# Stores ahead of casts on GpSimd, key casts later in one tile, and end stores on three queues, in a fused window-attention and MLP kernel

## The chip, the cores and the metric

The kernel runs on one core of one Trainium2 chip. The metric is device time in microseconds (us) of one execution; before the change it is 292.84, the median of three runs (292.73 to 294.62). A profiled execution of the same program took 293.94, of which the profile's span covers 292.2.

## The reference

What is computed is sliding-window attention over 8 batches of 8 heads (576 positions, 64 numbers per head, window of 32 to each side), followed by a two-layer network with a GELU on the 4608 tokens of 512 numbers that the attention gives. All inputs and the output are float32.

```python
scores = scale * np.matmul(q, k.transpose(0, 1, 3, 2))        # 8 x 8 x 576 x 576
mask = np.abs(pos[:, None] - pos[None, :]) <= 32
scores = np.where(mask, scores, -1000000000.0)
attn = softmax(scores)
x = np.matmul(attn, v).transpose(0, 2, 1, 3).reshape(4608, 512)
h = x @ w_in                                                  # 512 x 2048
g = 0.5 * h * (1.0 + np.tanh(c * (h + 0.044715 * h * h * h)))
return g @ w_out                                              # 2048 x 512
```

## The kernel before

The network's work is cut into nine tiles of 512 tokens, t = 0 to 8, and the attention into eight batches of 576 positions. They are interleaved by hand: while tile t's second product (`ffn_out`) runs on TensorE, the attention of batch b = t + 1 is placed between its matmuls, and the tile's first product with its GELUs (`ffn_in`, `in_mixed`) comes before it. Nothing is scheduled by a planner that weighs costs; each engine works off its instructions in the order in which the program records them, and a wait holds up everything behind it on that engine.

A tile's `ffn_out` is 112 matmuls, i = 0 to 111, in seven products n = 0 to 6 of 16 matmuls (a Strassen-Winograd scheme with seven products instead of eight). After the last matmul of a product VectorE (DVE) combines it into the output tile `yo`, at lines L804 (n = 0), L806 (n = 1), L808 (2), L816 (3), L819 or, in the last tile, L822 (4), L825 (5) and L834 (after n = 6). There is one `yo` for all tiles from 1 on, so a tile's L804 and L806 overwrite what the tile before has still to store. Rows 2 and 3 of `yo` are stored after L825, rows 0 and 1 after L834, by `store` (L755). A row is 128 tokens and is cut where its addresses in the output break, so one call gives two to five DMAs. All but the last tile's stores are issued by GpSimd (POOL); the last tile's go by SyncE (SP) and ScalarE (ACT), in turn within a call. In the built program SP's and ACT's DMAs use eight completion semaphores in turn, all POOL's another eight; a DMA waits until the one before it on its semaphore has landed. At its very end SP waits for the last use of each semaphore in a list.

The attention's steps are placed by tables, `PLAN` and its variants: each entry gives, for a matmul index i, the steps to record before it. `s0` to `s4` are scores of a head pair (4: the tails of all pairs, positions 480 to 575), `m` their masks (L511), `g`/`v` the sums and the products with the values, `x` the spread into `xT`, `a0` to `a3` the casts of the next batch's queries (L431) and `b0` to `b3` those of its keys (L441). After `b1` and `b3` SP issues a DMA transpose of two pairs of keys (L443). The mask of group 3, `m3`, stands at i = 70, that of the tails, `m4`, at 74, and the sums of groups 2 and 3, `g2`, at 88. Tile 0 has its own plan, tiles 1, 2 and 3 have `PLAN_1`, `PLAN_2` and `PLAN_L`, and tiles 4 to 6 have `PLAN`, in which `b0 b1` stand at i = 66 and `b2 b3` at i = 80. In `PLAN_L` they stand at 84 to 95.

Batch 3's values are loaded by SP into `vr` (L416) and cast by POOL into `V` in four casts (L1040), recorded in tile 1 before matmul 94; DVE pairs them (L236, L237) in tile 2 before they are used. The end of tile 1's product n = 5, and with it L825 and the stores of rows 2 and 3, comes at i = 95. At i = 98 batch 3's queries are cast (`open_and_turn`) and POOL casts its tail of queries and keys (L362, `cast_tails`). TensorE transposes that tail (L367, `trans_tails`) after column 12 of tile 2's first product, and ACT copies the result out (L369, L371). Columns 0 to 2 (`begun`) of a tile's first product are done at the end of the tile before.

Of the kernel before, what the change touches and what calls it, by code (L numbers as in the profile page):

```python
# [36 lines left out]
def cut(b):  # L37
# [8 lines left out]
PLAN = {7: "s0@0 s1@1 v-1", 16: "m0 m1 x-1", 35: "s2@0 g0@1", 38: "m2", 46: "x0 a0", 52: "x1 a1 a2 a3",  # L46
        63: "s3@0 s4@1", 66: "b0 b1", 70: "m3", 74: "m4", 80: "b2 b3", 88: "g2@1", 108: "x2", 112: "x3"}
# [5 lines left out]
PLAN_0 = {4: "s0@0", 9: "r1@1", 14: "s1@0", 15: "w1", 16: "m0", 19: "k2", 22: "r2@1", 23: "m1", 28: "s2@0 w2",  # L53
          29: "t-1@1", 34: "s-1@1 n0@0", 35: "e0", 36: "m2", 37: "k3", 38: "w5", 39: "m-1", 41: "w3 r3@1", 43: "e1 d0",
          47: "s3@0 v-1@1 d1 w4 e2 e3", 48: "d2 m3 d3", 50: "u3", 52: "x-1", 54: "n2@0",
          59: "p0@0 p2@1 x0 x1", 60: "e4 x2 x3", 61: "c1"}
# [12 lines left out]
PLAN_2 = {7: "s0@0 s1@1 v-1", 16: "m0 m1 x-1", 35: "s2@0 g0@1", 38: "m2", 46: "x0", 52: "x1",  # L69
          63: "s3@0 s4@1", 66: "a0 a1", 70: "m3", 74: "m4", 80: "a2 a3", 88: "g2@1", 108: "x2", 112: "x3"}  # L70

PLAN_L = {7: "s0@0 s1@1 v-1", 16: "m0 m1 x-1", 35: "s2@0 g0@1", 38: "m2", 46: "x0", 52: "x1",
          63: "s3@0 s4@1", 66: "a0 a1", 70: "m3", 74: "m4", 80: "a2 a3", 84: "b0", 88: "g2@1", 92: "b1", 95: "b2 b3", 108: "x2", 112: "x3"}

PLAN_1 = {12: "s0@0 s1@1 s2", 16: "m0 m1", 36: "m2", 56: "s-1@0 g0@1", 62: "m-1 x0", 64: "x1",
          80: "s3@0 g-1@1", 81: "m3", 90: "x2", 92: "x-1", 104: "v3 s4@1", 112: "x3 m4"}
# [6 lines left out]
LONE = 3  # L83
# [5 lines left out]
def kernel(  # L89
# [9 lines left out]
    nc = tc.nc  # L99
    B, H, S, D = q.shape  # L100
# [258 lines left out]
    def cast_tails(b, copy, half=slice(0, 128)):  # L359
        if len(halfs[b]) < 3:  # L360
            halfs[b].append(hp.tile([128, H, 64], FP16, name="t16", tag="t16"))
        copy(halfs[b][2][half, :, :], raws[b][2][half, :, :])  # L362
# [383 lines left out]
    def store(t, t4, yo, cols=slice(0, 512), *engs):  # L746

        m = i = 0
        while m < 128:
            b, c = divmod(t * 512 + t4 * 128 + m, S)  # L750
            q0, n = (0, cut(b)) if c < 4 * cut(b) else (cut(b), 144 - cut(b))
            j, p = divmod(c - 4 * q0, n)
            e = min(n - p, 128 - m)
            eng = engs[i % len(engs)] if engs else nc.gpsimd
            eng.dma_start(out_v[b, j, q0 + p:q0 + p + e, cols], yo[m:m + e, cols])  # L755
            m += e
            i += 1
# [16 lines left out]
    def ffn_out(t, i):  # L774

        n, blk, f = i // 16, i // 8 % 2, i % 8
        if n == 1 and t >= NT - 2:
            blk, f = divmod(i % 16, 4) if i % 16 < 8 else (i // 2 % 2, i // 4 % 4 * 2 + i % 2)
        a, w, new = WINO[n]
        end = t == NT - 1  # L780
        if i % 16 == 0 and new:
            pys[n % 2] = bank((1 + n) % 2)
            if end and n == 4:
                pys["apart"] = psO.tile([128, 512], FP32, name="py2", tag="O")
        py = pys[n % 2].rearrange("p (b c) -> p b c", b=2)
        apart = end and blk and n in (4, 6)
        if a[0] == "A":
            r0, c0 = 8 * (int(a[2]) - 1) + f, 256 * (int(a[1]) - 1) + 128 * blk
            lhsT = gTs[t][:, r0, c0:c0 + 128]
        else:  # L790
            lhsT = wino[a][:, f, 128 * blk:128 * blk + 128]
        one = end and n in (4, 6)
        nc.tensor.matmul(pys["apart"][:, 0:256] if apart else py[:, blk, :], lhsT,  # L793
                         wino[w][:, f, :], start=(new and i % (8 if one else 16) == 0),
                         stop=(i % (8 if one else 16) == (7 if one else 15)),
                         skip_group_check=True)
        if i % 16 < 15:
            return
        yo, left, right = wino["yo"], slice(0, 256), slice(256, 512)
        C11, C12, C21, C22 = (yo[:, r:r + 2, c] for r in (0, 2) for c in (left, right))  # L800

        M1, U2, U3 = C21, C12, C22
        if n == 0:
            (nc.scalar.copy if t >= NT - 2 else nc.vector.tensor_copy)(M1, py)  # L804
        elif n == 1:
            nc.vector.tensor_tensor(U2, py, M1, op=ALU.add)  # L806
        elif n == 2:
            nc.vector.tensor_copy(C11, py)  # L808
            if t >= NT - 2:
                for step in "z1 z2 z3".split():  # L810
                    sums(t, int(step[1]), PARTS[step[0]])
            if end:
                for x in range(2):
                    store(t, x, yo[:, x, :], left, nc.sync)
        elif n == 3:
            nc.vector.tensor_tensor(U3, py, M1, op=ALU.add)  # L816
        elif n == 4:
            if not end:
                nc.vector.tensor_tensor(C22, py, U3, op=ALU.add)  # L819
            else:  # L820
                for x, part in enumerate((py[:, 0, :], pys["apart"][:, 0:256])):
                    nc.vector.tensor_tensor(C22[:, x, :], part, U3[:, x, :], op=ALU.add)  # L822
                    store(t, 2 + x, yo[:, 2 + x, :], right, nc.sync, nc.scalar)
        elif n == 5:
            nc.vector.tensor_tensor(C21, py, M1, op=ALU.add)  # L825
            for x in range(2):
                store(t, 2 + x, yo[:, 2 + x, :], *((left, nc.sync, nc.scalar) if end else ()))

    def ffn_last(t):
        py = pys[0].rearrange("p (b c) -> p b c", b=2)  # L830
# [144 lines left out]
    for t in range(NT):  # L975
        b = t + 1
        att = b < B
        if t:
            for fc in range(begun):
                ffn_in(t, fc, 3, 4, then=False)  # L980
            for fc in range(begun):
                gelu(t, fc)
            if b == 2:
                open_and_turn(2)
                combine(2, nc.vector)
                combine(3, nc.vector)
            elif att:
                if t >= LONE:
                    in_x(t)
                if b == 3:  # L990
                    turn_keys(b)
            if t >= NT - 2:
                if t == NT - 2:
                    in_x(t)
                in_mixed(t)
            elif t >= LONE:
                in_mixed(t)
            for fc in range(begun, NF if t < LONE else 0):
                ffn_in(t, fc)
                if t == 1 and fc == 3:  # L1000
                    turn_keys(2)
                    load_vr(2)
                    raws[2] = [None, None, raws[2][2], vrs[2], tailp.tile([64, H, 64], FP32, name="vt", tag="vt")]
                    nc.sync.dma_start(raws[2][4], v[2, :, 512:S, :].rearrange("h p d -> p h d"))
                    raws[3] = rawp.tile([128, H, 256], FP32, name="qr", tag="q0")
                    load_q(3, raws[3])
                    combine(4, nc.vector)
                if t == 1 and 6 <= fc < 10:
                    cast_v(2, fc - 6)
                if t == 1 and fc == 6:  # L1010
                    trans_tails(1, psO.tile([128, 8, 128], FP16, name="pt", tag="O"))
                if t == 1 and fc == 8:
                    cast_tails(2, nc.scalar.copy)
                if t == 1 and fc == 13:
                    trans_tails(2, psO.tile([128, 8, 128], FP16, name="pt", tag="O"), copy=nc.scalar.copy,
                                copy_q=nc.scalar.copy)
                if t == 2 and fc == 12:
                    trans_tails(3, psO.tile([128, 8, 128], FP16, name="pt", tag="O"), copy=nc.scalar.copy,
                                copy_q=nc.scalar.copy)
                if t == 2 and fc == 8:  # L1020
                    pair_v(b, nc.vector.tensor_copy)
                if t == LONE - 1 and fc in (8, 9, 10, 11):
                    in_w(nc.vector, "B", (8, 9, 10, 11).index(fc) + 1)
        plan = PLAN_0 if not t else PLAN_1 if t == 1 else PLAN_2 if t == LONE - 1 else PLAN_L if t == LONE else PLAN if att else {16: "v-1", 40: "x-1"} if t == B - 1 else {}

        def group(g):
            return (b, g) if g >= 0 else (b - 1, 4)
# [6 lines left out]
        for i in range(113 if t else 65):  # L1034
            if t > 1 and i == {2: 40, 3: 56}.get(t, 4) and b + 1 < B:
                nc.gpsimd.tensor_copy(after, KLs[b % 2][:, 3, 0:1])
                load_v(b + 1)
            if t == 1 and i == 94:
                for c in range(4):
                    nc.gpsimd.tensor_copy(Vs[1][:, c, :, :], vrs[3][:, c, :, :])  # L1040
            if t == 1 and i == 98:
                open_and_turn(3)
                cast_tails(3, nc.gpsimd.tensor_copy)
            for act in plan.get(i, "").split():
                kind, at = act[0], int(act[act.index("@") + 1:]) if "@" in act else None
                g = int(act[1:].split("@")[0])
# [128 lines left out]
```

## Time and profile before

| | us |
|---|---|
| median of three runs | 292.84 (292.73 to 294.62) |
| profiled execution | 293.94 |
| its span | 292.2 |
| tile 1, L804 to L834 | 70.3 to 86.4 |
| tile 2, L804 to L834 | 101.5 to 116.2 |
| tile 4, L804 to L834 | 162.0 to 177.6 |
| last tile, DVE's last L834 | ends 288.33 |

The times of the tiles are where DVE's combining steps stand in the timeline. PE is TensorE's matmuls and PEld its weight loads, which overlap them; a small q behind an engine's name is its sequencer, which issues DMAs and waits for semaphores. In the timeline a line gives start and length in us, engine, line of the kernel, operation, what is written and read, how often, and in brackets the idle time of the engine before it and what ended that. In the chain of waits a line gives start, length and what was being done. In the rows by slices each digit is a fortieth of the span, 7.3 us.

The costliest groups of instructions are the matmuls of the first product (L600, 113.9 us in two groups), those of the second (L793), POOL's issues of stores (L755, 42.0 us in 77) and ACT's exponentials (L502, 29.5 us in 31). Of 36.70 MB read and 9.44 MB written, 97839 of 113792 packets are under 512 B.

### The profile page before, as it was taken

To read this page: it belongs to the slowest core of one execution; us is meant where nothing else is said; L and a number is where in the kernel's file an instruction comes from. 1 tells how busy PE (TensorE), PEld (TensorE's weight loads), DVE (VectorE), ACT (ScalarE), POOL (GpSimd) and SP (SyncE) were. 2 spreads that over 40 slices of the span, in tenths; PEclk is the share of its full clock that TensorE was granted. 3 is DMA by queue.
4 is the path that set the end of the run, shared out by engine and by line. 5 is a ranking of instruction groups with operands and counts; after the bars stand their busy time and mean duration, and the time that the engine had idled before them with its cause. 6 is when DMAs were issued, how large, how long until landed. Compare 5 with 4: busy or idle time off the path is not lost.

```text
span 292.2 us, 7443 instructions
## 1 busy us (share of the span) xinstructions
PE 283.3 (97%) x2993; PEld 197.0 (67%) x2993; DVE 225.5 (77%) x499; ACT 196.9 (67%) x323; POOL 92.7 (32%) x158
## 2 busy tenths in 40 slices
PE   8889999999999999999999989999999999999994
PEld 3535544557765677668866876688667877887783
DVE  4755377998897968798998778889888967875682
ACT  5875867878577865687658845895689577905800
POOL 3435324102318652505166108500800070016000
PEclk9999999999999999999999999999999999999999
DMA  7999998999999999869999998698820031005013
GB/s 219 276 372 399 358 311 201 246 195 187 272 222 195 261 217 192 220 156 217 134 185 248 179 162 185 193 180 126 186 45 2 2 87 61 0 3 144 0 43 103
DMA packets 113792, 51.01 MB, mean 175 GB/s; under 512 B 97839, under 2 KB 109615, under 8 KB 113502
## 3 DMA queue, kind: packets, MB, share of 16 engines
q1 hardware_dynamic: 89604, 38.77, 59.0%
q0 software_dynamic: 23088, 10.82, 23.1%
q10 hardware_dynamic: 1066, 0.96, 1.0%
q8 instruction: 23, 0.38, 0.6%
q14 instruction: 11, 0.09, 0.1%
HBM read 36.70 MB, written 9.44 MB: 158 GB/s over the span
## 4 chain that ended last, share of the span: by engine, by line
PE 82%; DMA 9%; SPq 5%; issue 1%; DVE 1%; POOL 0%; ACTq 0%; DVEq 0%
PE mm L793 29%; PE ph L600 17%; PE mm L600 14%; PE pu L656 7%; DMA kr<-in_k_dram 3%; PE ps_s L489 3%; PE py L765 3%; PE mm L765 2%; DMA wst<-in_moe_w_in_dram 2%; SPq L204 2%; DMA qr<-in_q_dram 2%; DMA V<-in_v_dram 1%; PE ps_od L516 1%; SPq L282 1%; PE ps_d L516 1%
## 5 line engine op out<-in xcount | busy, mean ns | idle before, releaser
L600 PEld LDWEIGHTS <-w_in 128*128 128x128 f16 x448 | 50.2, 113 | 39.6 <-POOL w_in L261 1.2
L755 POOL DMA_DIRECT2D out_dram<-y x77 | 42.0, 554 | 93.2 <-DVE y L825 75.3
L600 PE MATMUL ph<-xT,w_in 128*128 128x512 f16 x240 | 60.4, 379 | 0.6 <-POOL w_in L261 0.6
L793 PEld LDWEIGHTS <-s 128*128 128x128 f16 x512 | 49.4, 98 | 6.6 <-issue 0.4
L600 PE MATMUL mm<-xT,w_in 128*128 128x512 f16 x208 | 53.5, 379 | 0.0
L793 PE MATMUL mm<-t,s 128*128 128x256 f16 x376 | 44.9, 273 | 0.2 <-DVE y L806 0.2
L793 PEld LDWEIGHTS <-gT 128*128 128x128 f16 x384 | 36.2, 98 | 6.6 <-issue 0.3
L502 ACT ACTIVATE pe<-ps_s 128x960 f16<-128x960 f32 (+1 forms) x31 | 29.5, 974 | 14.2 <-PE ps_s L489 14.1
L793 PE MATMUL mm<-w_out,gT 128*128 128x256 f16 x256 | 32.6, 273 | 0.0
L741 DVE TENSOR_TENSOR s<-gT 128x512 f16<-128x512 f16 x64 | 26.9, 425 | 5.7 <-ACT gT L608 2.9
L608 ACT ACTIVATE gT<-mm 128x512 f16<-128x512 f32 x28 | 16.5, 599 | 21.6 <-PE mm L600 21.5
L608 ACT ACTIVATE gT<-ph 128x512 f16<-128x512 f32 x38 | 20.9, 606 | 6.6 <-PE ph L600 6.6
L114 ACT ACT_TABLE_LOAD x18 | 23.1, 1283 | 2.2 <-issue 1.9
L554 ACT ACTIVATE lt<-lt 128x480 f32<-128x480 f32 (+3 forms) x36 | 21.1, 585 | 1.1
L511 DVE TENSOR_TENSOR pe<-pe,band 128x960 f16<-128x960 f16 x28 | 18.1, 664 | 2.0 <-ACT pe L502 1.9
L704 ACT ACTIVATE gT<-ph 128x512 f16<-128x512 f32 x22 | 13.2, 600 | 4.8 <-PE ph L600 4.7
L793 PE MATMUL mm<-t,gT 128*128 128x256 f16 x128 | 16.2, 273 | 0.0
L526 PEld LDWEIGHTS <-V 128*64 128x64 f16 x520 | 12.6, 112 | 5.2 <-DVE V L237 1.3
L741 DVE TENSOR_TENSOR s<-s,gT 128x512 f16<-128x512 f16 x32 | 14.4, 450 | 1.1
L553 ACT ACTIVATE lt<-ps_od 128x480 f32<-128x480 f32 (+2 forms) x13 | 7.1, 546 | 11.6 <-PE ps_od L526 6.2
L793 PE MATMUL mm<-w_out,s 128*128 128x256 f16 x120 | 14.6, 273 | 0.0
L227 POOL DMA_DIRECT2D V<-in_v_dram x16 | 14.3, 912 | 0.5 <-PE mm L600 0.2
(153 smaller groups left out, 472.7 us busy)
## 6 DMA issues: line engine op xcount, KB each, us to landing
kr<-in_k_dram SPq DMA_DIRECT2D x31, 256.0 KB
qr<-in_q_dram SPq DMA_DIRECT2D x6, 1024.0 KB
wst<-in_moe_w_in_dram SPq DMA_DIRECT2D x8, 512.0 KB
vr<-in_v_dram SPq DMA_DIRECT2D x12, 256.0 KB
wst<-in_moe_w_out_dram SPq DMA_DIRECT2D x2, 1024.0 KB
wst<-in_moe_w_out_dram SPq DMA_DIRECT2D x4, 512.0 KB
V<-in_v_dram POOLq DMA_DIRECT2D x16, 128.0 KB, 8.2
qr<-in_q_dram SPq DMA_DIRECT2D x7, 256.0 KB
```

The costliest lines, as they stand in the source:

```text
L114: nc.scalar.add_instruction(mybir.InstLoadActFuncSet(name=nc.get_next_instruction_name(), act_func_set_id=which, ins=[], outs=[]))
L227: nc.gpsimd.dma_start(V[:, c, :, :], v[b, :, 128 * c:128 * c + 128, :].rearrange("h p d -> p h d"))
L502: nc.scalar.activation(pe, ps[:, :, 0:w], AF.Exp, scale=SCALE)
L511: nc.vector.tensor_tensor(pe, pe, m.rearrange("k (o j) p -> k o j p", o=1).broadcast_to(list(pe.shape)), op=ALU.mult)
L554: nc.scalar.activation(lt[:, 0:n], lt[:, 0:n], AF.Exp, scale=-1.0)
L600: nc.tensor.matmul(ph, w_cols[:, dc, fc // 4, fc % 4, :], xT[:, dc, t * 512 % RING:t * 512 % RING + 512], start=(dc == 0), stop=(dc == 3))
L608: nc.scalar.activation(gTs[t][:, fc, :], phs[fc], AF.Gelu_apprx_tanh)
L656: nc.tensor.matmul(ps[:, 256 * h:256 * h + 256], lhs[:, d, h, :], rhs[:, d, :], start=(n in (0, 2, 4) and h == d == 0), stop=(h == d == 1) ...
L741: nc.vector.tensor_tensor(dst, x, y, op=op)
L755: eng.dma_start(out_v[b, j, q0 + p:q0 + p + e, cols], yo[m:m + e, cols])
L765: nc.tensor.matmul(pys[t4], gTs[0][:, fc, t4 * 128:t4 * 128 + 128], w_out16[:, fc, :], start=new, stop=(fc == NF - 1))
L793: nc.tensor.matmul(pys["apart"][:, 0:256] if apart else py[:, blk, :], lhsT, wino[w][:, f, :], start=(new and i % (8 if one else 16) == 0) ...
```

## The change

It has three parts.

In tile 1 the four casts of batch 3's values move from i = 94 to i = 97, so that on POOL the four DMAs that store rows 2 and 3 of tile 1 (48, 80, 40 and 88 rows) come ahead of them. The cast of batch 3's tail moves from i = 98 of tile 1 into tile 2's first product, at column 3, so that on POOL it comes behind all stores of tile 1. The transposes of the tail move from after column 12 to after column 14.

Tile 4 gets a plan of its own, `PLAN_M`: `b0` moves from i = 66 to 84, `b1` to 92, `b2 b3` from 80 to 95. On DVE all four key casts then stand between L819 and L825; before, two stood ahead of the mask `m3` and two behind L819.

In the last tile the left halves of rows 2 and 3, after L825, go differently: row 2's two DMAs (40 and 88 rows) both by SP, row 3's five (32, 24, 24, 24, 24) by ACT and POOL in turn. Before, each row's were dealt to SP and ACT in turn.

Otherwise each engine's instructions and their order are the same; lines from L74 on move down by three, and later ones by up to six.

```diff
+PLAN_M = {7: "s0@0 s1@1 v-1", 16: "m0 m1 x-1", 35: "s2@0 g0@1", 38: "m2", 46: "x0 a0", 52: "x1 a1 a2 a3",
+          63: "s3@0 s4@1", 70: "m3", 74: "m4", 84: "b0", 88: "g2@1", 92: "b1", 95: "b2 b3", 108: "x2", 112: "x3"}
...
         elif n == 5:
             nc.vector.tensor_tensor(C21, py, M1, op=ALU.add)
             for x in range(2):
-                store(t, 2 + x, yo[:, 2 + x, :], *((left, nc.sync, nc.scalar) if end else ()))
+                store(t, 2 + x, yo[:, 2 + x, :],
+                      *((left, *((nc.scalar, nc.gpsimd) if x else (nc.sync,))) if end else ()))
...
-                if t == 2 and fc == 12:
+                if t == 2 and fc == begun:
+                    cast_tails(3, nc.gpsimd.tensor_copy)
+                if t == 2 and fc == 14:
                     trans_tails(3, psO.tile([128, 8, 128], FP16, name="pt", tag="O"), copy=nc.scalar.copy,
                                 copy_q=nc.scalar.copy)
...
-        plan = PLAN_0 if not t else PLAN_1 if t == 1 else PLAN_2 if t == LONE - 1 else PLAN_L if t == LONE else PLAN if att else {16: "v-1", 40: "x-1"} if t == B - 1 else {}
+        plan = PLAN_0 if not t else PLAN_1 if t == 1 else PLAN_2 if t == LONE - 1 else PLAN_L if t == LONE else PLAN_M if t == LONE + 1 else PLAN if att else {16: "v-1", 40: "x-1"} if t == B - 1 else {}
...
-            if t == 1 and i == 94:
+            if t == 1 and i == 97:
                 for c in range(4):
                     nc.gpsimd.tensor_copy(Vs[1][:, c, :, :], vrs[3][:, c, :, :])
             if t == 1 and i == 98:
                 open_and_turn(3)
-                cast_tails(3, nc.gpsimd.tensor_copy)
```

## The prediction, before the result was known

> **What bounds the kernel now.** First the page's busy times and slices:
>
> ```profile
> PE 283.3 (97%) x2993; PEld 197.0 (67%) x2993; DVE 225.5 (77%) x499; ACT 196.9 (67%) x323; POOL 92.7 (32%) x158
> ...
> PE   8889999999999999999999989999999999999994
> ...
> PEclk9999999999999999999999999999999999999999
> DMA  7999998999999999869999998698820031005013
> ```
>
> TensorE (PE) is busy 97% of 292.2 us at full clock and the chain of waits lies on it for 82%. An edit in the middle can gain only what PE loses to a wait; work shortened elsewhere is worth nothing. Listing PE's idle time from 60 us on leaves two gaps over 0.15 us, both DVE's doing, and then the end. The DMA row is full until 175 us, so a transfer put earlier pushes another.
>
> Gap one, the chain of waits at 153 to 177 us (start, length, what), tile 4:
>
> ```profile
> 157.83 3.96 SPq L204
> 161.79 0.04 issue
> 161.84 9.72 DMA kr<-in_k_dram
> ...
> 172.44 0.58 DVE pe L511
> 173.02 0.04 issue
> 173.06 0.39 PE ps_d L516 x2
> ```
>
> and DVE's timeline there:
>
> ```profile
> 169.70 0.69 DVE L816 TENSOR_TENSOR y<-mm,y 128x512 f32<-128x512 f32 x1
> 171.68 0.76 DVE L441 CAST k<-kr 128x512 f16<-128x512 f32 x2 [1.30 <-DMA kr<-in_k_dram]
> 172.36 0.65 DVE L511 TENSOR_TENSOR pe<-pe,band 128x960 f16<-128x960 f16 x1
> ```
>
> The key casts stand ahead of mask L511, so a mask whose scores ScalarE had exponentiated by 170.6 waits for keys that land at 171.56.
>
> Gap two, the timeline at 106 us (tile 2), POOL's at 87 to 99, and the DMA view's sizes with median us to landing:
>
> ```profile
> 105.84 0.69 DVE L806 TENSOR_TENSOR y<-mm,y 128x512 f32<-128x512 f32 x1 [1.95 <-DMA V<-in_v_dram]
> ...
> 106.59 0.38 PE L793 MATMUL mm<-t,s 128*128 128x256 f16 x2 [0.23 <-DVE y L806]
> ```
>
> ```profile
> 87.46 0.79 POOL L1040 CAST V<-vr 128x512 f16<-128x512 f32 x1 [5.85 <-DMA vr<-in_v_dram]
> ...
> 90.16 1.48 POOL L1040 CAST V<-vr 128x512 f16<-128x512 f32 x2 [0.36 <-DMA vr<-in_v_dram]
> 91.58 2.12 POOL L755 DMA_DIRECT2D out_dram<-y  x4
> ...
> 98.20 1.08 POOL L755 DMA_DIRECT2D out_dram<-y  x2 [0.90 <-DVE s L741]
> ```
>
> ```profile
> out_dram<-y POOLq DMA_DIRECT2D x1, 144.0 KB, 6.9
> ```
>
> L806 overwrites the output tile, so it waits for tile 1's stores, whatever load the profile names: the last one (72 rows, 144 KB) is issued at 98.75 and lands 6.9 us later, at 105.6.
>
> The end, SP's and ACT's last issues:
>
> ```profile
> 288.90 0.33 ACTq L755 DMA_DIRECT2D out_dram<-y  x1
> 289.26 0.32 SPq L755 DMA_DIRECT2D out_dram<-y  x1
> ```
>
> Their data are ready when DVE's last add ends, 288.33. SP waits 1.2 us more for the last landing (290.9), then works off its list of final waits; the span ends at 292.2.
>
> **Tile 4's keys late: -1.05 us.** Casts and their two transposes are kept; they move behind L819. Then: L816 ends 170.38, L511 and the tail's mask (0.65 and 0.55) end by 171.5, L819 (0.68; its matmuls end by 170.8) at 172.1, four casts at 0.34 us from one start to the next end at 173.5. The keys landed at 171.56, so they wait for nothing. PE's second sum, at 173.06, could start 0.22 us after the first (171.77, the spacing in tiles 3 and 5), at 171.99: 1.07 gained; I take 1.05. What is late next? L825, queued behind the casts: its matmuls would end at 174.94 - 1.07 = 173.87, the casts at 173.5, so 0.3 to 0.4 us of cover. The first key transpose on SP's queue follows the queries' one (ends 172.73) as now; the second goes at about 174.1 instead of 174.78. The next tile's scores come 17 us later. Bounds: 0, if the wait reappears at L825, to 1.19, the excess over the usual spacing of those starts.
>
> **Tile 2: -0.25 us net.** The four stores at L825 need only L825 (ends 83.34), so POOL, idle from 81.6 to 87.46, issues them at 83.6 and has 2.1 to 2.8 us of work (0.53 each here, 0.70 beside casts of DVE at 179 us): done by 86.4, before the first values land. Ahead of them in POOL's queue nothing waits; behind them are the casts. What it costs is DMA time: the queue is full, and 512 KB in the packets of these stores take 1.3 to 1.8 us of the 16 engines (the two 256 KB stores at 79.6 took 1.76). The four value loads, which landed at 87.4 to 90.8, thus come later by 0 to 1.8 us; I take d = 1.3, nearest the packets' undisturbed time. Casts end at 91.63 + d = 92.9. DVE's pairing copies of V, due at 94.12, still find them; SP's transposes behind the value loads slip by d too, and the first keys are needed only at 99.3 (landed 95.65), the second pair at 103 (98.82). Then seven stores (2.77 + 1.08 = 3.85) and only then the tail cast (0.61 to 0.88), which ends at 97.4 to 97.7. PE wants its four transposes after column 14, at 97.5 (97.72 less the 0.22 of transposes now at 95.77). Stall: 0 with d = 0, 0.7 with d = 1.8; I take 0.15. ScalarE's two copies out of them (0.37, 0.39) fit between its GELUs, idle 0.27 apart, and move the table load by at most 0.1.
>
> In return the 72-row store is issued at 95.0 + d and, even at 6.9 us, lands at 103.2, before L806 can start (103.89). PE's gap goes: 0.23 by the modelled ends, 0.40 by the weight load's idle time beside it; taken as 0.40. Net -0.25, from -0.4 to +0.5.
>
> **The end: -0.85 us.** Bytes and stores are the same, but the 11 DMAs after the last-but-one product (SP six, ACT five) become: SP 40, 88, 56, 48 rows; ACT 32, 24, 24, 72, 80; POOL 24, 24. In the built program the DMAs of SP and ACT share eight completion semaphores in turn, and each waits until the one eight before it has landed. Now the 48-row store goes at 289.26, held by a 24-row one issued at 287.23; the 80-row one goes at 288.90, held by the 88-row one issued at 286.88 (1.97 us before). With two DMAs gone to POOL's own semaphores the 48-row store depends on one issued at 285.67 and goes at 288.4 (data 288.33, SP has two issues fewer). The 80-row store depends on a 32-row one issued at 286.88; the 40-row one of that moment released its successor at 288.47, so 288.5 to 288.85. Last landing, 1.63 us after its issue as now (290.89 - 289.26): 290.2 to 290.5, or 290.85 with 1.97. Gain 0.45. Further, the last landing is now the first of SP's eight final waits, with seven behind it at 0.062 us; it becomes the eighth of nine, so 0.4 us less remains. Together 0.85, bounds 0.3 and 1.2. POOL's two stores are new here. DVE to POOL takes 0.3 us now (L825 ends 205.51, store 205.80): issues at 287.15 and 287.7; in the quiet stage at 262 us such stores land 1.9 to 2.7 us after issue, so by 290.4 at the latest, and SP waits for those first.
>
> The Trainium skill speaks against this part: "DMA: Bandwidth & Descriptors", Issuing engines are not separate DMA queues, says that DMAs from several engines run on the same 16 DMA engines and that this saves only the time to initiate them, usually small. By it the end would gain nearly nothing and the sum would be 1.3 (291.5); the trace disagrees so far, as waits for completions, and not only issuing, hold the last two.
>
> **Sum.** 1.05 + 0.25 + 0.85 = 2.15. The profiled execution took 293.94 (span 292.2 and 1.7 around it): 291.8 for it. It lies 1.10 above the median of 292.84, so 290.7 for the median. The shifts pass on: after both gaps the key loads start from casts that follow PE, and DMA has air at 120 to 127 and at 175 to 184 us, so nothing after them stays pinned to old times.
>
> **Rivals.** Tile 2 gives back more than it gets: d near 1.8, and PE stalls 0.7 at column 14. For it speaks the DMA share of 1.0 to 1.25 at 79 to 92 us; against it, POOL's stores share the engines and need not go first. That is +0.3 instead of -0.25: 291.3, chance 0.13.
>
> The transfers, not the issues, set the end: the 0.45 goes, and POOL's two stores take back part of the rest. Against it: the DMA share is 0.44 at 287 to 291 us. 291.2 to 291.6, chance 0.13.
>
> Tile 4's wait only moves: keys landing over 0.4 us later against PE make L825 late, and the adds behind it. Against it: tile 3 runs its casts in that place with no gap on PE. 291.4 to 291.8, chance 0.08.
>
> The two stalls are the profiled execution's own and hardly there in the median; then only the end remains: 292.0, chance 0.06.
>
> Slower than before: POOL's two stores land last. SP waits for them first, so with the 1.3 of the two tiles in hand a landing at 292.2 on the old clock (290.9 + 1.3; 4.5 us after the second issue) is where the change turns into a loss. At the full queue's 6.9 us it is 294.6, SP's end comes 3.7 later than now, and the time is 292.84 - 1.3 + 3.7 = 295.2. The quiet row (1.9 to 2.7) speaks against it. Chance 0.05.
>
> The forecast has 0.55, with 289.9 to 291.2 as its own range (all upper bounds together: 1.19 + 0.4 + 1.2 = 2.8). The range runs from 289.9 to 292.1 and leaves out the slower rival and mixtures. One per cent, what a measurement here can tell from no change, is 2.9 us: faster by more needs every part at its bound, 0.07; slower by more only the slow landing at its worst, 0.03; within, 0.90.
>
> **What would show it.** Right: in tile 4 DVE runs L511 directly after L816, L441 x4 after L819 without a wait, and the 0.90 gap before L516 is gone; L806 has no DMA wait; casts L1046 end at 92 to 93.5; the last SP issue lies at 288.3 to 288.5 on the old clock and POOL shows two issues after the last-but-one product. Wrong: a wait of L825 or of the transposes in column 14 over 0.5 us, or SP's final wait ending on POOL's stores.

## The result, and the profile after

The changed kernel takes 295.19 us (median of 22 runs, 293.96 to 297.10); the kernel before, in runs beside it, 293.96 (22 runs, 292.49 to 296.98). The ratio is 1.0042, 95% interval 1.0022 to 1.0061: about 1.2 us slower, where 2.15 faster was forecast. (The forecast's 290.7 was counted from a before of 292.84, so 1.1 of the 4.5 us from 290.7 to 295.19 is a difference between two medians of the kernel before.) The profiled execution took 294.83, of which the span is 293.1 (before 292.2). What follows goes through the same places as the prediction; lines from L74 on are 3 to 6 further down.

The page's busy times and slices. TensorE is as busy as before, so no work was added; two digits of its row differ from before: the 24th, at 168 to 175 us in tile 4, is 9 instead of 8, and the last is 1 instead of 4, which says that TensorE is done earlier relative to the span's end:

```profile
PE 283.1 (97%) x2993; PEld 196.8 (67%) x2993; DVE 225.6 (77%) x499; ACT 197.0 (67%) x323; POOL 94.4 (32%) x160
...
PE   8889999999999999999999999999999999999991
```

**Tile 4.** The chain of waits at 168 to 176 us (start, length, what), then VectorE's timeline:

```profile
169.31 2.84 PE mm L796 x25
172.14 0.32 PE ps_od L519 x2
172.46 0.20 PE ps_d L519 x2
...
173.13 2.73 PE mm L796 x24
```

```profile
170.00 0.69 DVE L819 TENSOR_TENSOR y<-mm,y 128x512 f32<-128x512 f32 x1
170.60 0.65 DVE L514 TENSOR_TENSOR pe<-pe,band 128x960 f16<-128x960 f16 x1
171.16 0.55 DVE L514 TENSOR_TENSOR pet<-pet,band 128x768 f16<-128x768 f16 x1
171.63 0.69 DVE L822 TENSOR_TENSOR y<-mm,y 128x512 f32<-128x512 f32 x1
172.23 1.43 DVE L444 CAST k<-kr 128x512 f16<-128x512 f32 x4
174.15 0.69 DVE L828 TENSOR_TENSOR y<-mm,y 128x512 f32<-128x512 f32 x1 [0.48 <-PE mm L796]
```

Before, the same last step stood at:

```profile
174.94 0.69 DVE L825 TENSOR_TENSOR y<-mm,y 128x512 f32<-128x512 f32 x1 [0.19 <-PE mm L793]
```

The chain no longer runs over the key loads, and the two sums (ps_od, ps_d) follow each other on TensorE without the gap. The mask runs directly after L819 and the four key casts wait for nothing; the step behind them, L828, waits for its matmuls only. From L819's start to L828's it is 4.15 us; before it was 5.24 (169.70 to 174.94): 1.09 gained.

**Tile 2.** GpSimd's timeline, then VectorE's at 104 us, then TensorE's at 98:

```profile
83.66 2.39 POOL L758 DMA_DIRECT2D out_dram<-y  x4 [1.35 <-DVE y L828]
...
92.16 0.88 POOL L1046 CAST V<-vr 128x512 f16<-128x512 f32 x1 [0.29 <-DMA vr<-in_v_dram]
92.99 3.98 POOL L758 DMA_DIRECT2D out_dram<-y  x7
96.97 0.98 POOL L365 CAST t<-tr 128x512 f16<-128x512 f32 x1
```

```profile
104.49 0.68 DVE L809 TENSOR_TENSOR y<-mm,y 128x512 f32<-128x512 f32 x1
```

```profile
98.00 0.40 PE L370 MATMUL pt<-idn,t 128*128 128x128 f16 x4 [0.48 <-POOL t L365]
```

The add that overwrites the output tile (L809, L806 before) waits for no store any more. But the casts of the values end at 93.04 instead of 91.64 and the tail cast at 97.95, so TensorE's transposes wait for it: 0.48 by the line's idle time, 0.65 by the distance of the starts over the usual one.

**The end.** The timeline from 285 us; SP's waits from 284 us on (waiting engine and line, released by: us in total, times, longest), after and then before; and the program's end on GpSimd by its source line (number of instructions: shortest, median and longest in ns, start of the first and of the last), after and then before:

```profile
286.35 1.00 POOL L758 DMA_DIRECT2D out_dram<-y  x2 [19.39 <-DVE y L828]
287.12 0.42 DVE L838 TENSOR_TENSOR y<-py,y 128x256 f32<-128x256 f32 x1 [0.45 <-PE py L796]
```

```profile
SPq L1175 <- PEq L1175: 2.9, 2, 2.4
SPq L1175 <- DMA out_dram<-y: 1.4, 1, 1.4
```

```profile
SPq L1170 <- DMA out_dram<-y: 1.2, 1, 1.2
...
SPq L1170 <- PEq L1170: 0.7, 2, 0.5
```

```profile
L1175 POOLq DRAIN  x3: 46/93/5564, 286.8 to 292.8; - x3
```

```profile
L1170 POOLq DRAIN  x3: 46/93/6027, 266.5 to 292.0; - x3
```

DVE's last add ends at 287.54 (before 288.33). SP's list of final waits is over at 290.02 (before 291.42), which is 2.48 after that add instead of 3.09. Then SP waits another 2.4 us, which the profile puts down to PE's sequencer, idle long before. The late one is GpSimd: at its own end stands a DRAIN, which begins at 286.8 and takes 5.56 us, to 292.33; the last barrier follows at 292.37. Before, the DRAIN began at 266.5, beside GpSimd's last stores, those of the tile before, and its 6.03 us were over at 272.56, under other work. So the span ends 5.56 after the last add, where it ended 3.91 after it before. GpSimd's two stores themselves landed at 288.46 and 289.25, ahead of the last landing of all, ScalarE's 80-row store at 289.86.

The three differences add up to the span's: +0.27 in tile 2, -1.09 in tile 4, +1.66 at the end, and with +0.03 ahead of them it is +0.87 in all (293.10 - 292.24, before rounding).

### The profile page after: what moved, and what is told of

Same layout as the page of the kernel before. It is cut to its first block, busy times and chain, and to the rows that moved or that the text cites. A ratio compares the mean times of both kernels' runs of the same rounds, so it can differ in the third digit from the quotient of the medians.

```text
span 293.1 us, 7444 instructions
## 1 busy us (share of the span) xinstructions
PE 283.1 (97%) x2993; PEld 196.8 (67%) x2993; DVE 225.6 (77%) x499; ACT 197.0 (67%) x323; POOL 94.4 (32%) x160
## 4 chain that ended last, share of the span: by engine, by line
PE 65%; POOL 1%; DVE 0%; issue 0%
PE mm L796 29%; PE ph L603 10%; PE mm L603 9%; PE pu L659 7%; PE ps_s L492 2%; PE ps_d L519 1%; PE mm L659 1%; PE ps_o L529 1%; PE ps_od L519 1%; PE ps_od L529 1%; PE py L796 1%; POOL out_dram L758 0%; POOL t L365 0%; DVE y L838 0%; PE pt L370 0%
## 5 line engine op out<-in xcount | busy, mean ns | idle before, releaser
L758 POOL DMA_DIRECT2D out_dram<-y x79 | 42.9, 551 | 111.4 <-DVE y L828 95.7
L492 PEld LDWEIGHTS <-KT 64*64 64x64 f16 x576 | 10.0, 106 | 6.1 <-issue 4.0
```

The costliest lines, as they stand in the source:

```text
L492: nc.tensor.matmul(sides[h][64 * half:64 * half + 64, 4 * n * r:4 * n * r + 4 * n].rearrange("k (j p) -> k j p", j=4)[:, :, p0 - q0:p1 - q ...
```

## The experiments

The theory was that GpSimd's DRAIN holds the end and is long because GpSimd issues stores shortly before; the rivals, that the other end stores are slow, that the middle lost the time, and that the DRAIN is long whatever GpSimd does last. Since the times of one kernel spread by several us from run to run, three lengths are read from each kernel's profiled execution beside the ratio: A, from the start of tile 1's L828 to that of tile 2's; B, tile 4's L819 to L828; C, from the end of the last add to the span's end.

| | A | B | C | ratio to before |
|---|---|---|---|---|
| before | 31.07 | 5.24 | 3.91 | |
| changed | 31.34 | 4.15 | 5.56 | 1.0042 (1.0022 to 1.0061) |
| 1 end without GpSimd | 31.90 | 4.14 | 4.38 | 0.9994 (0.9967 to 1.0021) |
| 2 end as before | 30.68 | 4.14 | 3.92 | 0.9993 (0.9965 to 1.0021) |
| 3 end alone | 31.54 | 4.93 | 5.57 | 1.0059 (1.0022 to 1.0095) |
| 4 late copy | 31.80 | 4.14 | 4.45 | one execution |
| 5 96 rows joined | 30.68 | 4.15 | 4.05 | 0.9996 (0.9964 to 1.0028) |
| 6 same, tail cast first | 30.67 | 4.15 | 3.97 | 0.9963 (0.9932 to 0.9995) |
| 7 joined, tile 2 as before | 31.80 | 4.15 | 4.11 | 0.9965 (0.9936 to 0.9994) |
| 8 copy at the very end | 31.34 | 4.14 | 5.93 | one execution |
| 9 joined, queues even | 30.68 | 4.14 | 4.24 | 0.9994 (0.9964 to 1.0024) |
| 10 tail first, end as before | 30.91 | 4.14 | 3.93 | 0.9966 (0.9933 to 0.9998) |
| 11 same, row 2 by SyncE | 30.69 | 4.15 | 3.92 | 0.9959 (0.9930 to 0.9989) |
| 12 same, rows joined by two | 30.69 | 4.14 | 5.36 | 1.0034 (1.0008 to 1.0060) |

Diffs are against the changed kernel unless another is named.

**1. The end without GpSimd's stores.**

```diff
-                      *((left, *((nc.scalar, nc.gpsimd) if x else (nc.sync,))) if end else ()))
+                      *((left, *((nc.scalar,) if x else (nc.sync,))) if end else ()))
```

> The change, but the five end stores of the last tile's row 3 all go by ScalarE's queue, none by GpSimd's. Theory (GpSimd's own drain at the end of the program, 5.6 us in the changed kernel's profile and done 5.0 us after its last DMA issue, holds the end by about 2.3 us): with no late DMA of GpSimd its drain is over before 285 us, the span ends about 2.3 us earlier than the changed kernel's 293.1, at 290.6 to 291.0, and the time is 1.2 to 1.7 us below the kernel before (ratio 0.994 to 0.996). Rival A (the other stores of the end, their new dealing to SyncE and ScalarE, are what is slow): the span stays within 0.5 of 293. Rival B (the stall of TensorE in tile 2 carries the loss): no change against the changed kernel, ratio 1.003 to 1.005.

The DRAIN was over at 272.04 and C fell from 5.56 to 4.38. But the span was 292.2, not 290.6 to 291.0, and the ratio 0.9994, not 0.994 to 0.996. Of the shortfall 0.56 is tile 2's longer wait (A, 31.90); for the rest SP's waits say why:

```profile
SPq L1175 <- DMA out_dram<-y: 2.6, 1, 2.6
```

With ScalarE issuing all five, its last two stores went at 288.53 and 288.95 (the last add ended at 287.79) and the last landed at 290.82, so SP's list was over 3.56 after the add instead of 2.48. Rival A falls, since the changed kernel's other stores were not slow; the two stores that GpSimd took off the other queues were a real gain, and its DRAIN took more than that back.

**2. The middle alone**, the end stores as before:

```diff
-                store(t, 2 + x, yo[:, 2 + x, :],
-                      *((left, *((nc.scalar, nc.gpsimd) if x else (nc.sync,))) if end else ()))
+                store(t, 2 + x, yo[:, 2 + x, :], *((left, nc.sync, nc.scalar) if end else ()))
```

> The parts of tile 2 and tile 4 as in the change, the end as before. Theory (the middle gains 0.79 us by the end of VectorE's last add, the loss comes from the end alone): the last add ends near 287.5 and the time is 0.7 to 0.9 us below the kernel before, ratio about 0.9973. Rival B (the middle costs in the median what it gains in the profiled execution, as the stall in tile 2 varies): ratio 0.999 to 1.004.

C is back at 3.92. The medians are 293.59 against 294.63, but the ratio, 0.9993, lies in the rival's range, and the interval does not tell 0.7 us from none. The last add ended at 288.57 and not near 287.5, because this execution was 1.74 later than the changed kernel's already at tile 1's L828. A and B are 1.5 shorter than in the profile of before, since here tile 2's transposes met no wait. That execution and the one without GpSimd's end stores have the same middle; TensorE's timeline of each, first this one, then the other:

```profile
99.10 0.39 PE L370 MATMUL pt<-idn,t 128*128 128x128 f16 x4
```

```profile
98.30 0.40 PE L370 MATMUL pt<-idn,t 128*128 128x128 f16 x4 [1.05 <-POOL t L365]
```

The wait in column 14 comes and goes with the execution.

**3. The end alone**, on the kernel before: only the diff of the end stores.

> The kernel before with the new end stores alone. Theory: the last add ends where it did (288.3), SyncE's list of final waits is done 0.6 us earlier, and GpSimd's drain ends 5.0 us after its last issue, which is about 0.8 us later than in the changed kernel: drain over at 293.1, span near 293.9, time 1.6 to 1.8 us above the kernel before, ratio 1.0055 to 1.006. Rival A (dealing and landings): SyncE's list itself ends later than before, with GpSimd's drain over ahead of it. Rival B (loss in the middle): ratio 0.997 to 0.999.

```profile
L1171 POOLq DRAIN  x3: 46/102/5564, 290.7 to 296.8; - x3
```

C is 5.57, 1.66 more than before, as in the changed kernel; GpSimd's last issue ended at 291.27, its DRAIN 4.97 later, and SP's list at 293.95, 2.49 after the add. This execution was 3 us longer elsewhere (span 297.0), but the ratio, 1.0059, is +1.7 us, the size of the step in C.

**4. A late copy by GpSimd, no late store.** On top of the first experiment:

```diff
+            if end:
+                nc.gpsimd.tensor_copy(after, yo[:, 3, 0:1])
```

> No store of GpSimd at the end, but a copy of one column by GpSimd behind the last add, so that its last instruction is as late as in the changed kernel and no DMA. Theory (the drain is long because of DMAs that GpSimd issued a short time ago): the drain after the copy is short, under 1 us, and the span is that of the kernel without GpSimd's late stores, 290.6 to 291.0. Rival C (whatever GpSimd does last, its drain then takes 5 us): drain over at about 293, span 293 to 294.

The timeline and GpSimd's end by its source line:

```profile
288.26 0.19 POOL L833 CAST after<-y 128x1 f16<-128x1 f32 x1 [19.21 <-DVE y L828]
```

```profile
L1177 POOLq DRAIN  x3: 46/102/5026, 288.2 to 293.8; - x3
```

The theory's reason fell: with no store of GpSimd for 19 us, the DRAIN still took 5.03 us, and was over at 293.27, 4.83 after the copy. It cost little here, as SP's list was over only 0.14 earlier (C is 4.45, against 4.38 in experiment 1). Rival C stands: the DRAIN is over about 5 us after GpSimd's last work of any kind.

**5. Fewer stores at the end.** 8 instead of 11 after the last-but-one product, none by GpSimd:

```diff
-                store(t, 2 + x, yo[:, 2 + x, :],
-                      *((left, *((nc.scalar, nc.gpsimd) if x else (nc.sync,))) if end else ()))
+                if end and x:
+                    q0 = cut(B - 1)
+                    nc.sync.dma_start(out_v[B - 1, 3, q0 - 32:q0, left], yo[0:32, 3, left])
+                    nc.scalar.dma_start(out_v[B - 1, :, q0:144, left], yo[32:128, 3, left])
+                else:
+                    store(t, 2 + x, yo[:, 2 + x, :], *((left, nc.sync, nc.scalar) if end else ()))
```

> Tiles 2 and 4 as in the change; at the end row 3's five stores become two (32 rows by SyncE, the other 96 rows in one store by ScalarE), none by GpSimd, so that 8 stores follow the last-but-one product instead of 11. Theory (GpSimd needs 4.8 to 5.0 us after whatever it does last, so its late work costs; and the last two stores of before are held by waits for stores eight earlier): the last stores are issued as soon as the last add is over, SyncE's list of final waits is over 2.4 to 2.6 us after that add, the span ends 3.2 to 3.4 us after it (before 3.9, changed kernel 5.6, run without GpSimd's stores 4.4). With the middle at -0.7 that is -1.3 against the kernel before, ratio about 0.9957. Rival (one store of 96 rows lands late, or the transfers set the end anyway): 3.9 us or more after the last add, ratio 0.997 or above.

**6. The same with the tail cast ahead of the seven stores.** The `cast_tails(3, ...)` goes back behind `open_and_turn(3)` at i = 98; the transposes stay at column 14.

> As the last kernel, but GpSimd's tail cast of tile 2 goes directly behind its four casts of V, ahead of the seven stores. Theory (TensorE's wait of 0 to 1.2 us in column 14 of tile 2, in four executions of the changed middle, comes from the tail cast behind the seven stores): the cast ends near 94 to 96 on the changed kernel's clock, the wait is gone; the 72-row store goes 0.6 to 1.0 later and the add that overwrites the output tile waits 0 to 0.5 us for it. Net 0.3 to 0.7 better on average than with the tail cast last: -1.6 to -2.0 against the kernel before, ratio 0.993 to 0.995. Rival (the transposes wait for something else, as the key loads): the wait in column 14 stays.

**7. The same end, with tile 2 as before:** the kernel before with `PLAN_M` and the joined store.

> The kernel before with tile 4's late key casts and the merged end stores; tile 2 as before. Theory (the edit of tile 2 costs 0 to 0.8 us, 0.3 on average, instead of gaining 0.25): 0.3 better than the merged kernel with tile 2 edited, -1.6 against the kernel before, ratio 0.9945, with tile 2's wait of the overwriting add back (gap on TensorE 0.4). Rival (tile 2's edit gains as predicted): 0.25 worse than the merged kernel with it, ratio 0.9965.

**8. A copy behind the last add**, on top of experiment 5:

```diff
+        if t == NT - 1:
+            nc.gpsimd.tensor_copy(after, yo[:, 1, 511:512])
```

> The merged kernel with one more instruction: GpSimd copies one column of the last rows behind the last add, with no DMA after it. Theory (GpSimd's drain is over 4.8 us after its last instruction, whatever that is): copy of 0.2 us starting 0.1 to 0.2 after the add, drain over 5.1 us after the add, span's end 5.9 to 6.0 after it: 2.6 more than without the copy. Rival (the drain's length belongs to the store descriptors that GpSimd writes; with none issued for 20 us it is short): the end stays 3.2 to 3.4 us after the add.

Joining failed: in 5 the last stores were issued 0.03 and 0.29 after the last add, without any wait, and still landed 2.76 and 2.94 after it (2.12 and 2.32 in the changed kernel), so C is 4.0 to 4.1 in 5, 6 and 7, where 3.2 to 3.4 was expected. An earlier issue is not an earlier landing.

The copy behind the last add came out as forecast, C 5.93:

```profile
287.32 0.19 POOL L848 CAST after<-y 128x1 f16<-128x1 f32 x1 [20.69 <-DVE y L842]
```

```profile
L1181 POOLq DRAIN  x3: 46/102/5026, 287.3 to 292.8; - x3
```

The copy ends at 287.51 and the DRAIN at 292.33, again 4.83 later, and 2.0 after SP's own list (290.35). No DMA of GpSimd is near.

With the tail cast first (6) the transposes had no wait and A was 30.67, though the seven stores came 0.6 later. Tile 2 as before (7) was no better off in this execution, since with tile 2 as before the transposes can wait for the tail cast too, here behind four stores:

```profile
96.77 0.40 PE L370 MATMUL pt<-idn,t 128*128 128x128 f16 x4 [0.94 <-POOL t L365]
```

The ratio of 7 is 0.3% under that of 5, within their intervals, while A in the two profiles differs by 1.1 the other way. So the expectation that tile 2's edit costs time on average is not borne out, nor the opposite.

**9. Even queues:** as 6, with the engines of the 96-row and the 32-row store exchanged.

> As the merged kernel with the tail cast first, but SyncE takes the 96-row store and ScalarE the 32-row one: SyncE 240 KB and ScalarE 272 KB after the last-but-one product, instead of 176 and 336. Theory (in the merged kernels ScalarE's queue, with 336 KB, is what lands last, 2.9 us after the last add, where the changed kernel's even queues landed 2.3 after it): the end shrinks to 3.3 to 3.5 us behind the last add, ratio 0.991 to 0.994. Rival (the single store of 96 rows is slow by itself, or the transfers together set the end): 3.9 or more again, ratio 0.995 to 0.997. In tile 2 no wait in column 14, as in the other run with the cast first.

C 4.24: evening out the bytes did not help. This execution also lost 0.56 on TensorE behind tile 3's L828. VectorE's timeline in tile 3:

```profile
143.69 1.43 DVE L444 CAST k<-kr 128x512 f16<-128x512 f32 x4 [0.94 <-DMA qt<-in_q_dram]
145.04 0.68 DVE L828 TENSOR_TENSOR y<-mm,y 128x512 f32<-128x512 f32 x1
```

Tile 3's plan has the four key casts in the place that `PLAN_M` gives them in tile 4. Here they waited for a load (the chain of waits names that of the keys, landed by 143.47) and held up L828 behind them. No other of the fourteen executions lost so much there.

**10. Tail cast first, end as before.**

> The change with the tail cast first in tile 2 and the end stores as in the kernel before. Theory (merging brought nothing, the end is 3.9 us behind the last add either way; tile 2 without its wait takes 30.7 us from the last add of the first product row to that of the next, against 31.1 to 31.8 in three executions of before): middle 1.3 to 1.6 shorter than before, ratio 0.994 to 0.9965. Rival (the wait in column 14 comes back with an unlucky landing of the values): ratio 0.996 to 0.999.

**11. The changed kernel's dealing on two queues:** as 10, with row 2 by SyncE and row 3 by ScalarE and SyncE in turn.

```diff
-                store(t, 2 + x, yo[:, 2 + x, :], *((left, nc.sync, nc.scalar) if end else ()))
+                store(t, 2 + x, yo[:, 2 + x, :], *((left, *((nc.scalar, nc.sync) if x else (nc.sync,))) if end else ()))
```

> As the last kernel, with the changed kernel's dealing of row 2 (both stores by SyncE) and row 3's five by ScalarE and SyncE in turn: GpSimd's two stores go to SyncE. It tells what the dealing brings without a third queue. Theory (the changed kernel's earlier landings came from the two stores that left the shared completion semaphores): with 11 stores on two queues the last ones wait again, the end is 3.8 to 4.4 us behind the last add, ratio 0.994 to 0.9975. Rival (it was the dealing of the 88-row store): 3.3 to 3.5, ratio 0.992 to 0.995.

C 3.93 and 3.92 with 11 stores on two queues, however dealt. In 11 ScalarE's 80-row store is not held any more (issued 0.3 after the add), but SyncE's 48-row store is, until 0.97 after it. TensorE's transposes had no wait in 6, 9, 10 and 11; in 10 the overwriting add waited, and A is 0.23 above the shortest.

**12. Joining by two,** so that nothing waits: as 11, with the four stores of 24 rows as two.

```diff
...
+                    nc.scalar.dma_start(out_v[B - 1, 3, q0 - 32:q0, left], yo[0:32, 3, left])
+                    for eng, j in ((nc.sync, 0), (nc.scalar, 2)):
+                        eng.dma_start(out_v[B - 1, j:j + 2, q0:144, left], yo[32 + 24 * j:80 + 24 * j, 3, left])
...
```

> As the last kernel (row 2's stores by SyncE, tail cast first), with row 3's four stores of 24 rows joined to two of 48 rows, one by SyncE and one by ScalarE: 9 stores behind the last-but-one product instead of 11, so that none of the last two waits for a store eight before it that is still on its way. Theory (in the run before, SyncE's last store, 48 rows, was issued 0.97 us after the last add because of that wait, and landed 1.6 us later, last of all; that wait is 0.6 of the end): issued 0.05 after the add, the last landing 2.1 to 2.4 after it instead of 2.6, end 3.4 to 3.6 instead of 3.9, ratio 0.993 to 0.996. Rival (joined stores and the transfers before them set the landing, as in the kernels with 96 rows in one): last landing 2.6 to 3.1 after the add, end 3.9 to 4.2.

Worse than theory and rival: the last landing came 4.4 after the last add, C is 5.36. The work by stretches (last two numbers: DMA share and GB/s), first this kernel, then experiment 11:

```profile
287.00:288.00 1.00, 0.00 (x0) 0.00 (x0) 0.00 (x0) 0.00 (x0) 0.00 (x0) 1.00 0.18 45
288.00:289.00 1.00, 0.00 (x0) 0.00 (x0) 0.00 (x0) 0.00 (x0) 0.00 (x0) 1.00 0.38 71
289.00:290.00 1.00, 0.00 (x0) 0.00 (x0) 0.00 (x0) 0.00 (x0) 0.00 (x0) 1.00 0.83 225
```

```profile
287.00:288.00 1.00, 0.00 (x0) 0.00 (x0) 0.00 (x0) 0.00 (x0) 0.00 (x0) 1.00 0.69 195
288.00:289.00 1.00, 0.00 (x0) 0.00 (x0) 0.00 (x0) 0.00 (x0) 0.00 (x0) 0.86 0.41 126
```

The last adds end alike, at 286.87 and 286.63, and the last stores are issued at 287.53 and 287.60. But with joined stores the DMA engines move little for two microseconds and then the rest in one. Each joined store also took 0.76 to 0.78 to issue, where 24 rows alone take 0.36 to 0.41.

The trace's records of the completion semaphores tell more. Leaving out one step soon after the issue, ahead of any landing, a store of 24 rows raises its semaphore in 12 steps as its parts land (experiment 11), the store that joins four stretches in 4 (experiments 5 to 9), and those that join two in 2. So a joined store seems to move in as many parts as it has stretches, here two of 24 KB instead of 12 of 2 KB. From issue to landing it takes 3.5 and 4.3 us with two stretches and 3.3 to 3.5 with four, against 1.9 to 2.0 for 24 rows in experiment 11. That this is what keeps the stores behind it back fits the low DMA share, but no run separates it.

## Why the prediction was wrong

**The step that failed** is the last of the end: "POOL's two stores are new here ... so by 290.4 at the latest, and SP waits for those first." It priced the landing of GpSimd's stores and put what GpSimd itself has to do behind them at nothing, without a reason. What it said of the stores came true. On the old clock (0.79 added) they were issued at 287.14 and 287.64 and landed by 290.04; SP's last issue was at 288.36, the 80-row one at 288.65, the last landing at 290.65, all within its bounds. SP's list came 0.61 nearer to the last add, against 0.85. But the program's end waits for each engine, and GpSimd is not done when its stores have landed: its DRAIN is over 4.97 after its last issue ends (changed kernel and experiment 3) or 4.83 after a copy (4 and 8). In the profile of before the same stretch, there 4.81, was over 20 us ahead of the end, where nothing showed it as a cost. What the row would have given: last issue ends 287.35, plus 4.8, is 292.2, 2.1 after SP's list. The end is +1.66 instead of -0.85, and these 2.5 us turn the forecast gain into a loss. All signs that the prediction named for being right were there; none of them was about GpSimd's own end. Of its signs for being wrong, the transposes' wait stood at the limit (0.48 or 0.65, against 0.5).

The rival for "slower" named the right engine and the wrong event: GpSimd's stores did not land last, its own end came last. That its 295.2 is next to the measured 295.19 is luck: it counts from a before of 292.84 and has 3.7 for a landing that came early. Of the other rivals, tile 2 giving back more (a stall near 0.7) was met in four of six executions of the changed middle. Tile 4's wait only moving was met in none, but tile 3 lost 0.56 that way in experiment 9, where the prediction took its casts for safe. And the stalls of before were no oddity of one profile: tile 4's shows in both executions that have it, and tile 2 waited in all three, twice for the overwriting add and in experiment 7 for the transposes.

**Tile 4: -1.05** was right. Between the two profiles it is -1.09; the other execution with before's tile 4 (experiment 3) has 4.93, so -0.8 to -1.1 against 4.14 to 4.15 in every kernel with `PLAN_M`. The cover that the prediction counted on held.

**Tile 2: -0.25 net.** The delay of the value loads, 1.3 taken, was 1.4 in the changed kernel's profile. But the seven stores took 3.98 instead of 3.85 and the tail cast 0.98 instead of 0.61 to 0.88. Both terms of the sum were too small. The shortest A of the changed middle is 30.68, without a wait of TensorE there, so what is above that is taken as waiting. The changed middle waited 0.66, 1.22, 0, 1.12, 0 and 0.66 in six executions, mean 0.61, where 0.15 was taken for column 14. Before's middle waited 0.39, 0.86 and 1.12 in three, mean 0.79, where 0.40 was taken from the only profile there was. The net, -0.18, is near the forecast, but by two errors that cancel, over few executions.

**The sum.** -0.94 (mean of tile 4) - 0.18 + 1.66 is +0.5. The medians say +1.2, from 0.65 to 1.8; between 0.1 and 1.3 of it has no place in the profiles. Where an execution stands when tile 1's L809 starts differs more than all that: 71.9 to 75.0 us over these fourteen profiles.

**The Trainium skill's rule** ("DMA: Bandwidth & Descriptors", Issuing engines are not separate DMA queues: issuing from several engines saves only the initiation) spoke against the end. SP's list did come 0.6 nearer to the last add, and experiments 1 and 11, with the same 11 stores on two queues, do not have that gain (3.56 and 3.10 after the add). Experiment 1 agrees with the rule: ScalarE's seven issues stand one behind another, the last 1.17 after the add instead of 0.32. In 11 SyncE's last store is issued 0.97 after the add, behind an earlier store's completion, in the changed kernel 0.03 after it; there the third queue saved such a wait, and not only initiation. Whether the gain is to be had on two queues stays open, as the joined stores of 5, 6, 7, 9 and 12 are slow to land by themselves.

**A faster kernel** is experiment 11: tile 4 as in the change, tile 2 with the tail cast directly behind the casts of the values, and nothing by GpSimd in the last tile. It took 292.71 against 294.16 for the kernel before, ratio 0.9959 (0.9930 to 0.9989); experiments 6, 7 and 10 are within its interval, so which of their parts brings it is not told apart.

## What to carry to other kernels

Before giving an engine late work, look at how that engine ends in the profile of before: the time from its last instruction to the end of its own closing instructions counts, even where it is now hidden. A gap seen in one profiled execution is one draw: where its length hangs on when loads land in a full queue, price it from several executions. And a store issued earlier, or joined with others, is a gain only if its landing moves too.

## What the runs showed of the hardware

GpSimd's DRAIN at the end of the program is over 4.81 to 4.97 us after its last work, in every profile here, after a store's issue and after a copy of one column alike. The other engines' DRAINs there are over sooner: in the changed kernel VectorE's 0.05 after its last add and ScalarE's 0.2 after its last issue, and SP's take 7 to 13 ns. The Trainium skill ("VectorE: DVE Perf Modes", The DRAIN you can't avoid) says that the DRAINs which the runtime puts before and after a kernel take a constant 12 ns or so on all five engines. Those here carry the closing line of the kernel itself (L1175), so the page need not mean them; SyncE's are as short, GpSimd's, with 5.0 to 6.1 us, are not.

A store whose rows go to two or four separate stretches of the output in one DMA landed 3.3 to 4.3 us after its issue, in two or four completion steps; one of 24 rows in one stretch 1.9 to 2.0 us, in 12 (experiment 11). With two joined stores the DMA share was 0.18 and 0.38 for 2 us.
